# Strassen's products for five pairs of tiles instead of three, and v of thirteen tiles read as float by SyncE

## The chip, the cores and the metric

The kernel runs on one core of one Trainium2 chip. The metric is the time of one execution in microseconds on the device. Engines are named as in the profile: PE (TensorE) multiplies matrices, DVE (VectorE) and ACT (ScalarE) work elementwise and read PSUM, POOL (GpSimd) works elementwise on SBUF and also issues the DMAs that change a type on the way, SP (SyncE) issues the other DMAs.

## The reference

The first half is a linear attention with decay (four batches, eight heads, 768 tokens, heads of 64), the second a feed-forward layer on the 3072 tokens of 512 numbers that come out of it:

```
for t in range(S):
    state = gamma * state + k[t] (outer) v[t]
    y[t] = q[t] @ state / sqrt(D)
x = y, heads side by side            # 3072 x 512
h = x @ w_in                         # 512 x 2048
g = h + sin(alpha * h)**2 / (alpha + 1e-9)
out = g @ w_out                      # 2048 x 512
```

## The kernel before, in words

The 3072 tokens are 24 tiles of 128. `order` is the order in which they are worked on, called P in the code: the first tile of each of the four batches, then the batches in turn. The tiles form ten groups (`sizes` is 4, eight times 2, then 4). Batch 1's last three tiles and the last five tiles of batches 2 and 3, thirteen in all, are "wide": their q, k and v are loaded for the whole batch at once, head by head, in `load_seq`, 64 tokens to a partition row. The other eleven are loaded tile by tile in `load_chunk`. All of these loads change float to bf16 and are issued by GpSimd.

For each tile v is scaled by a decay (`scale_v`, L184), q and k are transposed (`turn`, L294, a transposing DMA issued by SyncE), and the attention is done in chunks: a score matrix q k, masked on VectorE; a product with the state; a product of the masked scores with v; and a state update. `burst` does it for one tile, `pair` (L537) for two. In `pair` PE first writes the product with the state into the PSUM tile y (tag "two"), then the scores of the next tile into pa (tag "pa"), then the products with v into y, then scores of the tile after that into two banks of tag "mm". VectorE then masks pa, adds to the state, and takes y out in two exits, one per tile (`leave`, L560). PSUM has eight banks: four of tag "mm", two in tag "two", two in tag "pa".

The feed-forward part of a group runs in "phases". Phase g runs the up-projection of group g and the down-projection of group g - 1 side by side. A group of two tiles has eight slots in its phase. A `Slot` (L596) makes eight matmuls of 256 columns into a PSUM tile ph (two blocks of 128 of the 2048 hidden numbers, which the code counts as f = 0 to 15), ScalarE takes the sine, two activations, and the square, and VectorE adds s/alpha to ph and writes gT, the hidden numbers as bf16. The down-projection takes gT as the stationary operand and w_out as the moving one, 512 columns, 16 matmuls per tile into a bank po (`ff_out`, L631); VectorE copies po to SBUF and SyncE stores it. `phase` (L878) issues in each slot: the slot's matmuls and activations, what the last attention left to do, the attention at that slot (`atts`), the masks, a share of the down-projection, the slot's addition on VectorE, the second exit, the rest of the masks, and whatever is put behind the slot (`behind_slot`). Every engine works off its instructions in the program's order. The order of the first phases is written out by hand in `PLAN`.

Groups 8 and 9 are "fast" (L653): their down-projection is not done tile by tile. For a pair of tiles it is a product of two by two blocks (two tiles by two halves of the hidden numbers, with two halves by two halves of w_out), and the class `Seven` (L720) does it with Strassen's seven products instead of eight. A product is eight matmuls of 256 columns. The sums of blocks of w_out are made once by `mix_w` (L675; ten operations of 1024 columns), the sums of blocks of gT by `mix_g` (L687) in steps of three operations: s (sums), d (differences) and x, each for a part of the eight blocks m. The products are numbered 1 to 7: 4 and 3 take gT itself and add up in bank a; 5 and 2 take s and add up in bank b; 1 takes x and goes to bank c; 7 and 6 take d and add up further in bank a. Then VectorE (or ScalarE for the first) does: `hold`, a copy of b; `cross` (L783), a + b, stored as one half of the output; `rest` (L794), c - b; and `main` (L798), a + rest, the other half. `cross` has to read a before products 7 and 6 add to it. For group 8 banks a and b are the two halves of tag "two" and c is in "pa"; its pieces are spread evenly over the 16 slots of phase 9, which has no attention. Group 9 is done at the end by `fast_end`.

Buffers are shared by tag, each waiting for the last reader of what was there: gT has two buffers of 16 KB a partition; the ten buffers "qkr" hold q and k of a tile, later the sums of gT and some of w_out.

## Time and profile before

| what | value |
|---|---|
| median of 3 runs | 206.31 us (205.72 to 708.54) |
| the profiled execution, its own time | 207.02 us |
| its span, first to last instruction | 205.2 us |
| busy: PE, DVE, ACT, POOL | 195.2, 161.5, 151.8, 163.2 us |
| granted clock of PE | 0.997 of full speed |
| DMA queue of GpSimd | 80080 packets, 13.38 MB |
| DMA queues of SyncE and others in hardware | 23472 packets, 11.06 MB |

The page of the profile gives busy times per engine, a strip of the span in 40 slices, the chain of work that ended last, and groups of instructions by line. A row of a group has the line, the engine, the operation, output and input with their shapes, how often (x), busy time and mean of one, then the idle time before them and what ended it. Rows of a timeline have the start in the span, the duration, and the instructions merged. PE's matmuls overlap, so their starts tell more than their durations. Phase 6 starts at 122.33 us, phase 7 at 137.62, phase 8 at 152.92, phase 9 at 169.73. The rows of a stretch of time have the busy time of PE, PEld (loading of stationary operands), DVE, ACT and POOL with the count of each, then the clock, the DMA share and GB/s.

### The profile page before, as it was taken

To read this page: it belongs to the slowest core of one execution; us is meant where nothing else is said; L and a number is where in the kernel's file an instruction comes from. 1 tells how busy PE (TensorE), PEld (TensorE's weight loads), DVE (VectorE), ACT (ScalarE), POOL (GpSimd) and SP (SyncE) were. 2 spreads that over 40 slices of the span, in tenths; PEclk is the share of its full clock that TensorE was granted. 3 is DMA by queue.
4 is the path that set the end of the run, shared out by engine and by line. 5 is a ranking of instruction groups with operands and counts; after the bars stand their busy time and mean duration, and the time that the engine had idled before them with its cause. 6 is when DMAs were issued, how large, how long until landed. Compare 5 with 4: busy or idle time off the path is not lost.

```text
span 205.2 us, 6029 instructions
## 1 busy us (share of the span) xinstructions
PE 195.2 (95%) x2426; PEld 131.4 (64%) x2455; DVE 161.5 (79%) x344; ACT 151.8 (74%) x312; POOL 163.2 (80%) x204
## 2 busy tenths in 40 slices
PE   7889999999998999999999999999999999999993
PEld 7444544557765667666666676666766665555983
DVE  5787499877998887887998885995998775577853
ACT  7678888656996877877877959588586869999120
POOL 8998996999999996997399997999193876997000
PEclk9999999999999999999999999999999999999998
DMA  8999999999999999999996796994406101001123
GB/s 133 147 175 192 201 201 176 167 134 106 231 151 188 104 171 194 170 136 150 143 116 117 89 141 117 120 131 104 105 2 107 51 5 51 3 0 51 54 102 102
DMA packets 103580, 24.82 MB, mean 121 GB/s; under 512 B 93392, under 2 KB 101248, under 8 KB 103552
## 3 DMA queue, kind: packets, MB, share of 16 engines
q0 software_dynamic: 80080, 13.38, 92.8%
q1 hardware_dynamic: 23472, 11.06, 26.8%
q8 instruction: 19, 0.31, 0.7%
q14 instruction: 9, 0.07, 0.1%
HBM read 27.30 MB, written 6.29 MB: 164 GB/s over the span
## 4 chain that ended last, share of the span: by engine, by line
PE 83%; DMA 7%; POOL 4%; issue 2%; DVE 2%; ACT 1%; POOLq 0%
PE ph L610 37%; PE po L634 28%; DMA qkT<-qkr 4%; PE a L756 3%; DMA qkr<-in_q_dram 3%; PE ab L756 3%; POOL qkr L125 2%; PE b L756 2%; PE py L373 1%; POOL vr L125 1%; PE c L756 1%; PE pt L291 1%; PE pa L388 1%; PE py L437 1%; POOL w_in L161 1%
## 5 line engine op out<-in xcount | busy, mean ns | idle before, releaser
L625 DVE SCALAR_TENSOR_TENSOR gT<-s,rec_alpha,ph 128x256 bf16<-128x256 f32 (+3 forms) x164 | 79.4, 522 | 25.1 <-ACT s L618 24.6
L610 PE MATMUL ph<-xT,w_in 128*128 128x256 bf16 (+3 forms) x653 | 98.0, 291 | 0.3
L613 ACT ACTIVATE s<-ph,alpha_sb 128x256 f32<-128x256 f32 (+3 forms) x164 | 75.9, 505 | 28.1 <-PE ph L610 26.3
L610 PEld LDWEIGHTS <-w_in 128*128 128x128 bf16 x656 | 63.1, 98 | 29.6 <-DVE s_f L568 0.7
L634 PE MATMUL po<-w_out,gT 128*128 128x512 bf16 x264 | 70.3, 379 | 2.3 <-issue 1.9
L618 ACT ACTIVATE s<-s 128x512 f32<-128x512 f32 (+1 forms) x94 | 58.7, 626 | 2.8
L634 PEld LDWEIGHTS <-gT 128*128 128x128 bf16 x288 | 26.4, 98 | 20.8 <-DVE gT L625 0.5
L710 POOL TENSOR_TENSOR g_mix<-gT 128x512 bf16<-128x512 bf16 (+1 forms) x27 | 25.9, 994 | 7.2 <-DVE gT L625 7.2
L149 POOL DMA_DIRECT2D qk_seq<-in_q_dram x32 | 21.5, 712 | 6.6 <-DMA v_seq<-in_v_dram 6.1
L149 POOL DMA_DIRECT2D qk_seq<-in_k_dram x32 | 21.3, 720 | 1.5 <-DMA qk_seq<-in_q_dram 1.4
L149 POOL DMA_DIRECT2D v_seq<-in_v_dram x24 | 16.8, 743 | 0.0
L681 POOL TENSOR_TENSOR w_mix<-w_out 128x1024 bf16<-128x1024 bf16 x7 | 15.2, 2190 | 0.0
L756 PEld LDWEIGHTS <-g_mix 128*128 128x128 bf16 x128 | 11.9, 98 | 3.6
L644 DVE COPY o_sb<-po 128x512 f32<-128x512 f32 x15 | 10.3, 687 | 2.0 <-PE po L634 1.6
L125 POOL DMA_DIRECT2D vr<-in_v_dram x11 | 10.3, 932 | 1.2 <-DMA w_in<-in_moe_w_in_dram 0.7
L189 POOL TENSOR_TENSOR v_seq<-v_seq,kgq 128x512 bf16<-128x512 bf16 x9 | 9.8, 1097 | 1.4 <-DMA v_seq<-in_v_dram 1.4
L407 DVE TENSOR_TENSOR aTw<-pa,maskq 128x768 bf16<-128x768 f32 x10 | 9.5, 954 | 0.0
L495 DVE TENSOR_TENSOR xT<-py,qg 128x512 bf16<-128x512 f32 x13 | 8.9, 683 | 0.5 <-PE py L453 0.5
L869 PE MATMUL spare<-warm 128*128 128x112 bf16 (+1 forms) x52 | 7.9, 325 | 1.4 <-DVE warm L199 1.2
L391 DVE TENSOR_TENSOR aT<-pa,mask 128x1024 bf16<-128x1024 f32 x7 | 8.5, 1219 | 0.4 <-PE pa L388 0.4
L520 ACT CAST s_q<-s_f 128x256 bf16<-128x256 f32 x13 | 5.1, 393 | 2.7 <-DVE s_f L515 2.7
L165 POOL DMA_DIRECT2D w_out<-in_moe_w_out_dram x8 | 5.8, 727 | 1.2 <-DMA w_in<-in_moe_w_in_dram 0.8
(138 smaller groups left out, 217.7 us busy)
## 6 DMA issues: line engine op xcount, KB each, us to landing
out_dram<-o_sb SPq DMA_DIRECT2D x21, 256.0 KB, 3.9
w_in<-in_moe_w_in_dram POOLq DMA_DIRECT2D x8, 256.0 KB, 8.3
w_out<-in_moe_w_out_dram POOLq DMA_DIRECT2D x8, 256.0 KB, 7.9
vr<-in_v_dram POOLq DMA_DIRECT2D x11, 128.0 KB, 5.3
v_seq<-in_v_dram POOLq DMA_DIRECT2D x16, 80.0 KB, 4.7
qkr<-in_q_dram POOLq DMA_DIRECT2D x7, 128.0 KB, 6.4
qkr<-in_k_dram POOLq DMA_DIRECT2D x7, 128.0 KB, 5.8
qk_seq<-in_q_dram POOLq DMA_DIRECT2D x16, 48.0 KB, 4.4
```

Of the source, the lines that this page charges most:

```text
L125: nc.gpsimd.dma_start(out=t, in_=chunk_of(src, j))
L149: nc.gpsimd.dma_start(out=o, in_=src[bt, head(b, m, e), now[0] * C:(now[-1] + 1) * C, :].rearrange("(f i) d -> i f d", i=64))
L189: eng.tensor_mul(t, t, by[:, j % NCH, :, None].to_broadcast([128, H, D]))
L610: nc.tensor.matmul(self.ph[:, m, :], w_in[:, i, f * 128:(f + 1) * 128], xT[g][:, i, self.lo:self.hi], start=(m == 0 and i == 0), stop=(i = ...
L613: nc.scalar.activation(out=self.s[:, m, :], in_=self.ph[:, m, :], func=ACTF.Sin, scale=alpha_sb[:, f:f + 1])
L618: nc.scalar.activation(out=self.s, in_=self.s, func=ACTF.Square)
L625: nc.vector.scalar_tensor_tensor(gT[self.g][:, f, self.lo:self.hi], self.s[:, m, :], rec_alpha[:, f:f + 1], self.ph[:, m, :], op0=ALU.mult ...
L634: nc.tensor.matmul(po[g, ts], gT[g][:, f, ts * C:(ts + 1) * C], w_out[:, f, :], start=(f == 0), stop=(f == FF - 1))
L644: nc.vector.tensor_copy(o_sb, po[g, ts])
L681: eng.tensor_tensor(w_mix[n, i], w_block(*a, js), w_block(*b, js), op=op)
L710: eng.tensor_tensor(o, i0, i1, op=op)
L756: nc.tensor.matmul(t, self.left(n, j), r, start=k not in self.begun, stop=(j == FH - 1), skip_group_check=True)
```

## The change

1. v of the thirteen wide tiles is read as float, without a change of type, by SyncE. It goes into a new tile vf (16 rows of 256 floats), which takes the tag "gA". Groups 0 and 9, of four tiles, put their gT there too (one buffer of 16 KB); the groups of two keep "gT", two buffers of 8 KB. So vf lies where group 0's gT was, and group 9's gT comes after it. Batch 1 has the first six rows; batches 2 and 3 have the last ten, one after the other. `scale_v` now reads vf and writes the bf16 v. Batch 1's loads come right after PLAN, batch 2's in phase 3, batch 3's in phase 5, in SyncE's queue between transposes and stores.
2. The scalings move: those of tiles 9, 10, 11 and 13 go from VectorE to GpSimd, that of tile 17 comes earlier.
3. Groups 6 and 7 become fast as well: five pairs (groups 6, 7, 8 and two in group 9). Their `mix_g` steps are all on GpSimd, four steps of three operations each, behind slots 1, 3, 5 and 7 of their own phase.
4. Which products run in which slot is written out for groups 6 and 7. Group 6 (in phase 7, with a pair's attention in slot 4): bank a in "mm", banks b and c in "two"; `hold` on ScalarE in slot 3, `cross` and the first half of product 7 in slot 4, product 1 in slots 6 and 7. Group 7 (in phase 8, with a pair's attention in slot 1 and bursts in slots 4 and 6): all banks in "mm"; `hold` in slot 4, `cross` in slot 5, `rest` in slot 6.
5. The sums of w_out are made earlier, in phases 2 to 4: ten halves (512 columns) into the rooms "vr" of early v, seven on VectorE and three on GpSimd; five whole ones on GpSimd, into the rooms of the decay table and of batch 1's q and k.

The diff, cut to its core:

```
 def load_seq(...):
+        if "v" in names and "vf" not in raw:
+            raw["vf"] = work.tile([128, 16, NP, D], F32, name="vf", tag="gA", bufs=1)
...
+            if name == "v":
+                vf = raw["vf"][:, 16 - nh:16] if nh > 6 else raw["vf"][:, 0:nh]
+                for i, c in enumerate(cs):
+                    raw["vf", bt * NCH + c] = vf[:, 2 * i:2 * i + 2]
...
-                nc.gpsimd.dma_start(out=o, in_=...)
+                (nc.sync if name == "v" else nc.gpsimd).dma_start(out=o, in_=...)

 def scale_v(j, eng):
         t, by = raw["v", j], kg
+        o = t
         if wide(j):
-            t, by = t.rearrange("i f p d -> i (f p) d"), kgq
-        eng.tensor_mul(t, t, by[:, j % NCH, :, None].to_broadcast([128, H, D]))
+            o, t = (x.rearrange("i f p d -> i (f p) d") for x in (t, raw["vf", j]))
+            by = kgq
+        eng.tensor_mul(o, t, by[:, j % NCH, :, None].to_broadcast([128, H, D]))

-                gT[g] = work.tile([128, FF, n], BF16, name="gT", tag="gT", bufs=2)
+                gT[g] = work.tile([128, FF, n], BF16, name="gT", tag="gA" if sizes[g] == 4 else "gT", bufs=1 if sizes[g] == 4 else 2)

-    fast = (8, 9)
+    fast = (6, 7, 8, 9)

+    w_todo = {"vr": [(n, j, 2) for n in (7, 6) for j in range(0, FH, 2)] + [(1, 4, 2), (1, 6, 2)],
+              "dec": [(4, 0, 4), (4, 4, 4)], "seq": [(3, 0, 4), (3, 4, 4), (1, 0, 4)]}
+    def mix_w(eng, home):
+        n, i, c = w_todo[home].pop(0)
...
+        eng.tensor_tensor(to, w_block(*a, slice(i, i + c)), w_block(*b, slice(i, i + c)), op=op)

 class Seven:
+        def steps(self, *parts):
+            return [fn for part in parts for fn in ([part] if callable(part) else self.pieces(part))]

 def fast_pieces(g):
+        if g == NG - 3:
+            s = Seven(g, 0, lambda k: psum.tile([128, 2, NH], F32, name=k, tag="mm", bufs=4)[:, slice(0, 2) if k != "c" else 0])
+            parts = [[(4, range(7))], [(4, range(7, FH)), (3, range(6))], [(3, range(6, FH)), (5, range(5))],
+                     [(5, range(5, FH)), (2, range(4))], [(2, range(4, FH)), s.hold], [s.cross, (1, J)], [s.rest, (7, J)],
+                     [(6, J), s.main]]
+            return [s.steps(*p) for p in parts]
+        if g < NG - 3:
+            def between(k):
+                if k == "a":
+                    return psum.tile([128, 2, NH], F32, name=k, tag="mm", bufs=4)
+                return psum.tile([128, 2, 512], F32, name=k, tag="two")[:, 0].rearrange("p (x n) -> p x n", x=2)[:, slice(0, 2) if k == "b" else 0]
+            s = Seven(g, 0, between)
+            parts = [[(4, J)], [(3, J)], [(5, J)], [(2, J), s.hold], [s.cross, (7, range(4))], [(7, range(4, FH)), (6, range(3))],
+                     [(1, range(7))], [(1, range(7, FH)), s.rest, (6, range(3, FH)), s.main]]
+            return [s.steps(*p) for p in parts]

 def phase(...):
+        plan = outs if outs and isinstance(outs[0], list) else None
...
+            for fn in plan[n] if plan else ():
+                fn()

     load_seq(1, "q", between=P[8])
     load_seq(1, "k")
+    load_seq(1, "v")
     load_chunk(P[10], "v")
-    load_seq(1, "v")
     load_seq(2, "q")
+    scale_v(P[11], nc.gpsimd)
+    scale_v(P[12], nc.gpsimd)
     load_seq(2, "k")
-    load_seq(2, "v")
+    scale_v(P[13], nc.gpsimd)
     load_seq(3, "q", slice(0, 2))
     load_seq(3, "k", slice(0, 2))
-    for j in P[15:17] + P[18:19]:
-        scale_v(j, nc.gpsimd)

     def last_loads():
-        mix_w(nc.gpsimd)
         nc.gpsimd.tensor_copy(seen, st["qkT", P[17]][:, 0, 0:1])
         load_seq(3, "v")
-        mix_w(nc.gpsimd)
-        mix_w(nc.gpsimd)
+        load_seq(3, "q", slice(2, None))
         scale_v(P[17], nc.gpsimd)
-        load_seq(3, "qk", slice(2, None))
+        load_seq(3, "k", slice(2, None))

+    at((3, 3), lambda: load_seq(2, "v"))
+    for spot in ((2, 4), (2, 6), (3, 1), (3, 2), (3, 3), (3, 4), (3, 6)):
+        mixes(spot, lambda: mix_w(nc.vector, "vr"))
+    for spot in ((3, 4), (3, 5)):
+        mixes(spot, lambda: mix_w(nc.gpsimd, "dec"))
+    for i, spot in ((14, (3, 6)), (15, (4, 0)), (16, (4, 1)), (18, (4, 2)), (20, (4, 3))):
+        mixes(spot, lambda j=P[i]: scale_v(j, nc.gpsimd))
+    for spot in ((3, 7), (4, 1), (4, 2)):
+        mixes(spot, lambda: mix_w(nc.gpsimd, "vr"))
+    for _ in range(3):
+        mixes((4, 5), lambda: mix_w(nc.gpsimd, "seq"))
+    for g in (6, 7, 8):
+        for m in range(0, FH, 2):
+            mixes((g, m + 1), lambda g=g, m=m: mix_g(g, m, 2, nc.gpsimd))
```

Here (g, n) is slot n of phase g, NG is 10, J is all eight blocks of a product.

More of the change, by code (lines that the diff above doesn't have):

```diff
@@ L147, in load_seq @@
                 r, at = half(b), 2 * m + e
[L148 to L149 removed]
+                o = vf[r, fs, at, :] if name == "v" else tqk[r, fs, "qk".index(name), at, :]
+                (nc.sync if name == "v" else nc.gpsimd).dma_start(out=o, in_=src[bt, head(b, m, e), now[0] * C:(now[-1] + 1) * C, :].rearrange("(f i) d -> i f d", i=64))
         for i, c in enumerate(cs):
@@ L743, in right @@
                 return w_out[:, j + FH * (n == 5), NH * (n == 5):NH * (n == 5) + NH]
-            return w_mix[n, j // 4][:, j % 4]
+            return w_mix[n, j]
         def mm(self, n, j, half=None):
@@ L878, in phase @@
     def phase(g, outs, att, nf=1, on_vector=(), tags={}, early=()):
-        no, done = len(outs), 0
+        plan = outs if outs and isinstance(outs[0], list) else None
+        no, done = 0 if plan else len(outs), 0
         for n in range(FF // nf):
```

38 lines of the change are left out of this document (13 added, 25 removed).

## The prediction

> **What bounds the kernel now.** I read the page first, then PE's busy time by stretches.
>
> ```profile
> span 205.2 us, 6029 instructions
> PE 195.2 (95%) x2426; PEld 131.4 (64%) x2455; DVE 161.5 (79%) x344; ACT 151.8 (74%) x312; POOL 163.2 (80%) x204
> ```
> ```profile
> 60.00:80.00 20.00, 18.39 (x277) 12.91 (x279) 17.65 (x37) 15.30 (x33) 17.34 (x27) 1.00 1.80 161
> ```
>
> TensorE is busy 95% of the span; even the stretch from 60 to 80 us leaves it only 20 - 18.39 = 1.6 us idle. So the time is what PE executes plus what it waits, and relieving another engine buys nothing by itself. What matters is whether PE stays fed where the change touches it: phases 7 and 8, in which groups 6 and 7 go through w_out. The timeline of PE around the pair block of phase 7 comes next (start, duration, instruction).
>
> ```profile
> 142.84 1.04 PE L610 MATMUL ph<-xT,w_in 128*128 128x256 bf16 x8
> 143.71 1.03 PE L634 MATMUL po<-w_out,gT 128*128 128x512 bf16 x4
> 144.57 1.04 PE L610 MATMUL ph<-xT,w_in 128*128 128x256 bf16 x8
> 145.54 0.42 PE L544 MATMUL y<-qkT,s_q 64*64 64x128 bf16 x16
> ...
> 145.96 0.30 PE L421 MATMUL pa<-v_seq,qk_seq 64*64 64x64 bf16 x16
> ...
> 146.84 1.04 PE L634 MATMUL po<-w_out,gT 128*128 128x512 bf16 x3
> ...
> 152.92 1.04 PE L610 MATMUL ph<-xT,w_in 128*128 128x256 bf16 x8
> ```
>
> Slot 3 starts at 142.84, slot 4 at 144.57, the pair's attention at 145.54, phase 8 at 152.92: each starts where the last one ends. Nothing there waits today.
>
> **The products saved.** From 143.71 to 144.57 four passes of 512 columns take 0.86 us, 0.2155 each. The chain of waits has the Strassen passes of 256 columns:
>
> ```profile
> 197.70 1.75 PE a L756 x16
> ```
>
> That is 0.1094 each. A pair needs 32 of the first (6.90 us) or 56 of the second (6.13 us): 0.77 us saved, 1.55 for both pairs. This has one answer. All else is whether it survives.
>
> **Group 6 in phase 7: three new waits.** Slot 3 ends with product 2 and `hold`, ScalarE's copy of bank b; slot 4 has the pair's attention, then `cross`, then product 7 into the bank that `cross` reads; slot 6 opens bank c. Both b and c take the PSUM tag "two", which the pair's y takes as well. The rows that price it, ScalarE's and then VectorE's timeline, then the groups by form:
>
> ```profile
> 144.78 0.63 ACT L618 ACTIVATE s<-s 128x512 f32<-128x512 f32 x1
> ```
> ```profile
> 145.44 0.87 DVE L625 SCALAR_TENSOR_TENSOR gT<-s,rec_alpha,ph 128x256 bf16<-128x256 f32 x2
> 146.32 0.96 DVE L407 TENSOR_TENSOR aTw<-pa,maskq 128x768 bf16<-128x768 f32 x1
> 147.19 0.41 DVE L568 TENSOR_TENSOR s_f<-s_f,pa 128x256 f32<-128x256 f32 x1
> 147.52 0.87 DVE L625 SCALAR_TENSOR_TENSOR gT<-s,rec_alpha,ph 128x256 bf16<-128x256 f32 x2
> ...
> 151.11 0.68 DVE L561 TENSOR_TENSOR xT<-y,qg 128x512 bf16<-128x512 f32 x1
> ```
> ```profile
> L765 ACT COPY b_sb<-b 128x512 f32<-128x512 f32 x2 | 1.2, 585 | 5.2 <-PE b L756 5.2
> L791 DVE TENSOR_TENSOR o_sb<-a,b_sb 128x512 f32<-128x512 f32 x1 | 0.7, 691 | 2.2 <-ACT b_sb L765 2.2
> ```
>
> First, `hold` is queued on ScalarE behind slot 3's square, which ends at 144.78 + 0.63 = 145.41, and lasts 0.585: bank b is free at 146.0. The pair's first matmul, at 145.54 today, needs it: 0.45 us. Bounds 0 and 0.6.
>
> Second, the pair ends at 146.84 + 0.45 = 147.29. VectorE's mask needs the scores and the state sums in pa, ended at 145.96 + 0.30 + 0.45 = 146.71, so it runs then; the state addition follows 0.87 later at 147.58 (147.19 - 146.32), and `cross` 0.33 after that (147.52 - 147.19), at 147.91, since it comes behind both in program order. It ends 0.69 later at 148.60. Product 7 must not write what `cross` still reads: PE stands from 147.29 to 148.60, 1.31 us, with slot 5's matmuls and through them ScalarE queued behind. Bounds 0, were product 7 free of `cross`, and 1.6.
>
> Third, from the addition at 147.52 to the end of the pair's second exit at 151.11 + 0.68 VectorE's chain is 4.27 us today; now it starts at 148.60, so y is released at 152.87. PE does four passes (0.44), slot 5 (0.87), seven passes (0.77) and slot 6 (0.87), which makes 151.55, and finds c not free: 1.32 us. Bounds 0 and 1.9.
>
> The three make 3.1 us. Phase 7 becomes 3.1 - 0.77 = 2.3 us longer; what ends last there is VectorE behind the pair.
>
> **Group 7 in phase 8.** Its banks a, b and c all come from the four of tag "mm". A ph bank is held from 142.84 to the end of its addition, 145.44 + 0.87: 3.47 us. While b lives (slots 2 to 4) two banks are left for slots that come every 0.87 + 7 x 0.109 = 1.63 us, so the same bank is wanted after 3.26: about 0.2 us late, once, as the attention in slots 1, 4 and 6 stretches the others. `cross` stands a whole slot ahead of product 7 here. I take 0.25 us, bounds 0 and 1: so -0.5 net.
>
> **GpSimd.** It issues 24 fewer loads of v; it gains 24 combinations (eight steps of three) and four scalings; the sums of w_out move earlier. Rows: groups, then GpSimd's timeline, then the loads of v by tile.
>
> ```profile
> L710 POOL TENSOR_TENSOR g_mix<-gT 128x512 bf16<-128x512 bf16 x18 | 20.4, 1156 | 7.2 <-DVE gT L625 7.2
> L149 POOL DMA_DIRECT2D v_seq<-in_v_dram x24 | 16.8, 743 | 0.0
> L681 POOL TENSOR_TENSOR w_mix<-w_out 128x1024 bf16<-128x1024 bf16 x7 | 15.2, 2190 | 0.0
> L189 POOL TENSOR_TENSOR v_seq<-v_seq,kgq 128x512 bf16<-128x512 bf16 x9 | 9.8, 1097 | 1.4 <-DMA v_seq<-in_v_dram 1.4
> L710 DVE TENSOR_TENSOR g_mix<-gT 128x512 bf16<-128x512 bf16 x6 | 2.3, 417 | 0.0
> L577 POOL CAST s_q<-s_f 128x512 bf16<-128x512 f32 x2 | 1.4, 694 | 4.5 <-DVE s_f L572 4.5
> ```
> ```profile
> 107.88 3.05 POOL L189 TENSOR_TENSOR v_seq<-v_seq,kgq 128x512 bf16<-128x512 bf16 x3
> ...
> 125.08 1.04 POOL L189 TENSOR_TENSOR v_seq<-v_seq,kgq 128x512 bf16<-128x512 bf16 x1 [1.41 <-DMA v_seq<-in_v_dram]
> 126.06 5.31 POOL L149 DMA_DIRECT2D qk_seq<-in_q_dram  x8
> ...
> 158.22 2.90 POOL L710 TENSOR_TENSOR g_mix<-gT 128x512 bf16<-128x512 bf16 x3 [3.52 <-DVE gT L625]
> ```
> ```profile
> DMA to landing us min/median/max: 2.7/5.1/8.9
> ```
>
> Its first block of loads ends at 107.88 today; without 16 issues of v (11.9 us), with three of the new scalings among them (3.3), at about 99, some us less where waits on v go. Then come five whole sums of w_out (10.9), three halves (3.3) and five scalings (5.5): about 119. The last loads follow: eight of q (5.3) to 124, the scaling of tile 19 when v has landed (125.08 today; I keep that, SyncE having the loads now), and eight of k to 131.4. Only then do group 6's steps start. To the first operation of its last step stand three steps (8.7), a scaling (1.1), the state copy (0.7) and 1.16: 143.1. Product 5 in slot 2 reads it as its seventh pass, at 142.84 - 0.87 + 6 x 0.109 = 142.6. I take 0.5 us. Below: 0, as PE cannot gain from an early one; above: v landing at its 8.9 in place of 5.1, 3.8 more, 4.3. Phases 7 and 8 then ask GpSimd for 4 x 2.9 plus two scalings and a copy, 14.5 us of some 15, so it catches up by phase 9.
>
> GpSimd takes 1156 ns for what VectorE does in 417, 2.8 times. The Trainium skill, GPSIMD Engine Reference, section Engine selection, speaks against this choice: two-input elementwise work belongs on VectorE, GpSimd being some two times slower. By that factor a step would be about a quarter shorter and the 0.5 us would vanish; by the rows it stays.
>
> **SyncE and the loads of v.** SyncE's timeline, and the first use of a wide tile's transposes:
>
> ```profile
> 60.62 0.66 SPq L960 DMA_DIRECT2D out_dram<-o_sb  x1
> 69.16 1.23 SPq L297 DMA_TRANSPOSE qkT<-qk_seq  x1
> ```
> ```profile
> L395 PEld LDWEIGHTS <-qkT x104: 106/108/111, 78.0 to 162.1; 64*64 64x64 bf16 x104
> ```
>
> The first eight loads of v fall into SyncE's gap from 61.3 to 69.16; group 0's gT is dead by then, its last store (60.62) being issued ahead of them. Queued behind them: the transposes of tile 9, wanted at 78.0, and group 1's stores. The gap of 7.9 us takes eight issues at 0.66 (5.3). I take 0, bounds -0.3 (GpSimd's q and k queue gets shorter) and 3. The other sixteen come with 10 us or more ahead of their use. The scalings and sums taken from VectorE, and the three additions per pair that it gets instead of two copies, cost nothing but the waits above.
>
> **Sum.** 3.1 + 0.25 + 0.5 - 1.55 = +2.3 us on the span of 205.2, so 207.5; the profiled execution took 207.02 with what lies around the span, 0.7 above the median of the runs, 206.31. On the median: 208.6.
>
> **Rivals.** (a) The saving comes through: `cross` or the exits don't hold PE, for instance because VectorE, with fewer scalings, reaches them sooner. Against it: VectorE has no gap from 145.44 to 147.52, and each of these comes when PE's own scores are done. It gives -1.55 + 0.25, so 205.0. (b) Slower: GpSimd becomes the bound in phase 7. Its place is the seventh pass of product 5; it decides from 142.6 on, each us later is a us of the kernel, up to 4.3 in place of 0.5: 212.4. For it: the chain from 107.88 has no slack left in it; against: the waits on v that go. (c) SyncE's queue: v's packets ahead of tile 9's transposes make PE stand at 78.0, up to 3 us: 211.6. The Trainium skill, DMA: Bandwidth & Descriptors, section Queues, rings and completion order, says that descriptors of one queue are taken in ring order; no row of before shows such a load ahead of a transpose. (d) The change does not lower PE's work, for instance as 256-column passes pair badly with matmuls of other shapes: 0.1094 was measured at the end of the kernel alone; then +1.55 more, 210.2.
>
> Chances: the forecast 0.52, (a) 0.25, (b) 0.14, (c) 0.05, (d) 0.04. The point is the forecast's. The forecast's own range is 207 to 210.5. The low end takes in (a), 204.8; the high end most of (b) and (c), 212. About 2% (4.1 us) is what a measurement can tell from no change. Faster needs under 202.2: the whole saving and 2.5 us of waits that no row promises, 0.03. Slower needs over 210.4: most of (b) and (c), half of (d), a little of the forecast's tail, 0.22. Within: 0.75.
>
> **What would show it.** In the timeline of PE of after: idle before the pair's y with ScalarE's b_sb as the releaser (0.4), before product 7 with VectorE's o_sb (1.3), before product 1 with VectorE's exit (1.3), and before product 5 with GpSimd's g_mix (0.5); phase 8 lasting about half a us less than the 16.8 from 152.92 to the start of phase 9:
>
> ```profile
> 169.73 1.03 PE L610 MATMUL ph<-xT,w_in 128*128 128x512 bf16 x4
> ```
>
> PE without those gaps, or a gap before 100 us, would make the prediction wrong.

## The result, and the profile after

The changed kernel takes 220.07 us (median of 4 runs, 217.30 to 223.24) against 206.37 us before: a ratio of 1.063, with a 95% interval of 1.0497 to 1.0764. It is clearly slower. A few executions of a kernel come out slower than its others, and the ratios here and below leave these out (708.54 of before, 223.24 of after), so they are not quite the quotients of the medians, and e6's profile is of such an execution. The profiled execution took 217.3 us, with a span of 215.5 us, 10.3 more than the 205.2 before.

The length of a phase is read here from ScalarE's timeline: from the first square (L626; L618 before) of one phase to the first of the next. In the kernel after, phase 7 runs from the first of these rows to the second, 23.9 us:

```profile
141.91 0.63 ACT L626 ACTIVATE s<-s 128x512 f32<-128x512 f32 x1
...
165.81 0.63 ACT L626 ACTIVATE s<-s 128x512 f32<-128x512 f32 x1
```

| us | phase 2 | 3 | 4 | 5 | 6 | 7 | 8 |
|---|---|---|---|---|---|---|---|
| before | 15.89 | 15.67 | 15.58 | 16.31 | 14.99 | 15.30 | 16.64 |
| after | 14.82 | 17.91 | 15.67 | 16.32 | 16.09 | 23.89 | 16.10 |

The page after, in the lines that answer to those of before, and the busy times of 60 to 80 us:

```profile
span 215.5 us, 6176 instructions
...
PE 197.4 (92%) x2479; PEld 137.4 (64%) x2503; DVE 164.0 (76%) x346; ACT 153.0 (71%) x314; POOL 172.4 (80%) x209
```
```profile
60.00:80.00 20.00, 17.58 (x269) 12.21 (x271) 18.91 (x37) 15.22 (x33) 17.19 (x24) 1.00 1.98 177
```

PE is idle for 18.1 us of the span where it was for 10.0 before, and its share fell from 95% to 92%: 8.1 of the 10.3 us are waiting. The other 2.2 are PE being busy longer. From phase 9 on nothing moved (18.67 us to the last square in both). So 8.6 of the 10.3 us are in phase 7, 2.2 and 1.1 in phases 3 and 6, and phases 2 and 8 give back 1.1 and 0.5. From 60 us on, the rows of PE's timeline with a wait of over 0.3 us (in brackets: the idle time and what ended it) say who was late:

```profile
78.56 0.30 PE L454 MATMUL py<-aT,vr 64*64 64x128 bf16 x8 [1.57 <-DVE vr L197]
...
79.31 0.25 PE L403 MATMUL pa<-qkT 64*64 64x128 bf16 x4 [0.38 <-DMA qkT<-qk_seq]
...
132.93 0.37 PE L445 MATMUL y<-aTw,v_seq 64*64 64x128 bf16 x16 [0.67 <-POOL v_seq L197]
...
146.84 0.39 PE L764 MATMUL b<-w_out,g_mix 128*128 128x256 bf16 x2 [1.73 <-POOL g_mix L718]
149.66 0.39 PE L764 MATMUL b<-w_out,g_mix 128*128 128x256 bf16 x2 [2.42 <-POOL g_mix L718]
...
156.99 0.60 PE L764 MATMUL a<-w_mix,g_mix 128*128 128x256 bf16 x4 [1.35 <-DVE o_sb L799]
...
161.56 0.94 PE L764 MATMUL c<-w_mix,g_mix 128*128 128x256 bf16 x7 [1.46 <-DVE xT L569]
```

The last two are the waits for `cross` and for bank c, as forecast. The two before them are product 5 waiting for GpSimd's sums, 4.15 us together. Behind them PE also ran slower; the column before the last two is the granted clock:

```profile
140.00:150.00 10.00, 5.84 (x51) 4.52 (x50) 4.16 (x9) 5.19 (x11) 10.00 (x12) 1.00 0.22 54
...
150.00:160.00 10.00, 8.65 (x164) 6.90 (x161) 5.46 (x12) 5.00 (x10) 8.63 (x10) 0.83 0.23 54
```

Read by the microsecond, the clock is 0.50 to 0.52 from 150 to 153 us, right behind the two waits, and PE is busy all that time: it cost 1.7. Phase 7 then is 15.30 - 0.77 + 4.15 + 1.35 + 1.46 + 1.7 = 23.2. Most of the other 0.7 belongs to the waits too. A wait is counted from the end of the last matmul, but matmuls overlap: the four passes at 144.51 take 0.60 us, where a next one that was free would start 4 x 0.1094 = 0.44 us after them. So a wait costs up to 0.17 us more than its idle time, some 0.6 for the four (an estimate from such rows).

Why GpSimd was late is in the chain of waits, followed back from 149.66 (start, us, what):

```profile
112.25 6.26 POOL w_mix L687 x3
118.51 0.14 POOL seen L1122
...
118.66 0.63 SPq L155
...
121.47 1.90 SPq L155
...
123.42 1.11 SPq L155
...
125.75 5.96 DMA vf<-in_v_dram
...
131.83 1.04 POOL v_seq L197
...
138.40 2.91 POOL g_mix L718 x3
...
149.66 0.39 PE b L764 x2
```

It goes back to SyncE's loads, and they were late in two ways. They started late: batch 3's eight loads of v are issued from 118.66 on, while GpSimd issued them from 113.67 in the kernel before:

```profile
113.67 5.76 POOL L149 DMA_DIRECT2D v_seq<-in_v_dram  x8
```

In SyncE's queue they stand behind tile 16's transposes, whose issue ends at 118.12, and the chain has the first of them behind GpSimd's small copy `seen`, which comes after three whole sums of w_out. And they took longer: the first four issues take some 0.65 us each, the later ones 1.1 to 1.9, and the last load lands at 131.71. From the first issue to the scaling of tile 19 it is 13.17 us, against 125.08 - 113.67 = 11.41 before. So of the 6.75 us by which that scaling was late, 5.0 are the start and 1.8 the loads. GpSimd, which stands still for 7.93 us for that load, scales tile 19 at 131.83 instead of 125.08 before, issues k, and begins group 6's steps at 138.32. SyncE's three batches of such loads:

```profile
60.98 6.20 SPq L155 DMA_DIRECT2D vf<-in_v_dram  x8
...
80.31 12.49 SPq L155 DMA_DIRECT2D vf<-in_v_dram  x8
...
118.66 8.29 SPq L155 DMA_DIRECT2D vf<-in_v_dram  x8
```

And VectorE's timeline in phase 3, then GpSimd's: the scaling of tile 8 for which PE waited at 78.56 took 2.75 us, where the same operation took 0.68 before, and GpSimd made two scalings beside it.

```profile
75.76 2.75 DVE L197 TENSOR_TENSOR vr<-vr,kg 128x512 bf16<-128x512 bf16 x1
```
```profile
75.89 2.05 POOL L197 TENSOR_TENSOR v_seq<-vf,kgq 128x512 bf16<-128x512 f32 x2
```

The transposes of tile 9, for which PE waited at 79.31, were issued at 73.85, 4.7 us later than before. SyncE's queue was free of v from 67.18 on; what SyncE waited for was batch 1's k. In this stretch the median from issue to landing of GpSimd's q and k loads is 5.9 us, where it was 4.1.

### The profile page after: what moved, and what is told of

Its sections match the earlier page's. It is cut to its first block, busy times and chain, and to the rows that moved or that the text cites. A ratio compares the mean times of both kernels' runs of the same rounds, so it can differ in the third digit from the quotient of the medians.

```text
span 215.5 us, 6176 instructions
## 1 busy us (share of the span) xinstructions
PE 197.4 (92%) x2479; PEld 137.4 (64%) x2503; DVE 164.0 (76%) x346; ACT 153.0 (71%) x314; POOL 172.4 (80%) x209
## 4 chain that ended last, share of the span: by engine, by line
POOL 39%; PE 31%; DMA 16%; DVE 4%; SPq 3%; ACT 3%; issue 2%; POOLq 0%; DVEq 0%
PE ph L618 14%; POOL w_mix L687 6%; PE a L764 5%; POOL g_mix L718 4%; POOL qkr L123 4%; POOL qkr L125 4%; DMA qk_seq<-in_q_dram 4%; DMA w_in<-in_moe_w_in_dram 4%; POOL qk_seq L155 4%; POOL vr L125 4%; PE po L642 4%; POOL v_seq L197 3%; DMA vr<-in_v_dram 3%; SPq L155 3%; DMA vf<-in_v_dram 3%; PE b L764 3%
## 5 line engine op out<-in xcount | busy, mean ns | idle before, releaser
L618 PE MATMUL ph<-xT,w_in 128*128 128x256 bf16 (+3 forms) x652 | 98.9, 292 | 0.4
L618 PEld LDWEIGHTS <-w_in 128*128 128x128 bf16 x656 | 63.7, 98 | 26.7 <-issue 0.7
L626 ACT ACTIVATE s<-s 128x512 f32<-128x512 f32 (+1 forms) x94 | 58.7, 626 | 2.9
L642 PE MATMUL po<-w_out,gT 128*128 128x512 bf16 x206 | 54.8, 379 | 2.0 <-issue 1.6
L718 POOL TENSOR_TENSOR g_mix<-gT 128x512 bf16<-128x512 bf16 (+1 forms) x51 | 49.1, 1008 | 6.6 <-DVE gT L633 5.3
L642 PEld LDWEIGHTS <-gT 128*128 128x128 bf16 x224 | 20.6, 98 | 16.5 <-DVE gT L633 0.5
L764 PEld LDWEIGHTS <-g_mix 128*128 128x128 bf16 x208 | 19.8, 100 | 12.9 <-POOL g_mix L718 4.7
L155 POOL DMA_DIRECT2D qk_seq<-in_k_dram x32 | 21.3, 697 | 1.9 <-DMA qk_seq<-in_q_dram 1.6
L197 POOL TENSOR_TENSOR v_seq<-vf,kgq 128x512 bf16<-128x512 f32 x13 | 13.6, 1054 | 7.9 <-DMA vf<-in_v_dram 7.9
L687 POOL TENSOR_TENSOR w_mix<-w_out 128x1024 bf16<-128x1024 bf16 (+1 forms) x8 | 14.0, 1760 | 0.0
L764 PE MATMUL b<-w_out,g_mix 128*128 128x256 bf16 x64 | 9.5, 292 | 4.2 <-POOL g_mix L718 4.2
L125 POOL DMA_DIRECT2D vr<-in_v_dram x11 | 10.3, 934 | 1.0 <-DMA w_in<-in_moe_w_in_dram 0.7
L764 PE MATMUL a<-w_mix,g_mix 128*128 128x256 bf16 (+1 forms) x72 | 8.2, 261 | 1.4 <-DVE o_sb L799 1.4
L764 PEld LDWEIGHTS <-gT 128*128 128x128 bf16 x88 | 7.9, 98 | 2.2 <-DVE gT L633 0.3
L764 PE MATMUL a<-w_mix,gT 128*128 128x256 bf16 (+1 forms) x72 | 8.7, 261 | 0.0
```

Source lines behind the costliest of these rows:

```text
L125: nc.gpsimd.dma_start(out=t, in_=chunk_of(src, j))
L155: (nc.sync if name == "v" else nc.gpsimd).dma_start(out=o, in_=src[bt, head(b, m, e), now[0] * C:(now[-1] + 1) * C, :].rearrange("(f i) d ...
L197: eng.tensor_mul(o, t, by[:, j % NCH, :, None].to_broadcast([128, H, D]))
L618: nc.tensor.matmul(self.ph[:, m, :], w_in[:, i, f * 128:(f + 1) * 128], xT[g][:, i, self.lo:self.hi], start=(m == 0 and i == 0), stop=(i = ...
L626: nc.scalar.activation(out=self.s, in_=self.s, func=ACTF.Square)
L642: nc.tensor.matmul(po[g, ts], gT[g][:, f, ts * C:(ts + 1) * C], w_out[:, f, :], start=(f == 0), stop=(f == FF - 1))
```

## The experiments

Eighteen kernels, e1 to e18 in the order in which they ran ("the seventh run" is e7). Each row has the median in us, the ratio to the kernel before with its interval, the span of the profiled execution, and the lengths of its phases, read as above.

| run | median | ratio [95%] | span | 2 | 3 | 4 | 5 | 6 | 7 | 8 |
|---|---|---|---|---|---|---|---|---|---|---|
| e1 | 217.07 | 1.050 [1.043, 1.057] | 215.8 | 15.82 | 17.87 | 15.67 | 16.31 | 20.56 | 18.11 | 16.10 |
| e2 | 210.40 | 1.019 [1.012, 1.025] | 208.7 | 14.62 | 19.53 | 15.67 | 16.32 | 15.94 | 15.30 | 16.64 |
| e3 | 218.13 | 1.060 [1.051, 1.068] | 215.5 | 15.75 | 17.52 | 15.67 | 16.32 | 22.50 | 16.84 | 16.10 |
| e4 | 218.15 | 1.055 [1.047, 1.063] | 216.9 | 15.38 | 19.71 | 15.68 | 16.33 | 22.31 | 15.93 | 16.10 |
| e5 | 212.28 | 1.029 [1.020, 1.038] | 210.4 | 15.35 | 19.49 | 15.67 | 16.32 | 14.87 | 18.19 | 16.13 |
| e6 | 223.90 | 1.084 [1.077, 1.091] | 224.4 | 15.72 | 24.75 | 15.67 | 16.31 | 16.75 | 23.92 | 16.10 |
| e7 | 214.78 | 1.041 [1.034, 1.048] | 213.5 | 15.57 | 24.60 | 15.67 | 16.32 | 14.87 | 15.93 | 16.10 |
| e8 | 232.03 | 1.126 [1.117, 1.136] | 231.3 | 14.62 | 21.10 | 15.68 | 19.74 | 24.41 | 25.22 | 16.15 |
| e9 | 215.34 | 1.044 [1.039, 1.049] | 212.8 | 14.62 | 15.67 | 21.81 | 16.31 | 17.14 | 15.93 | 16.09 |
| e10 | 227.57 | 1.100 [1.092, 1.107] | 226.3 | 15.47 | 17.16 | 26.17 | 16.32 | 14.87 | 23.92 | 16.12 |
| e11 | 213.94 | 1.037 [1.033, 1.042] | 212.1 | 15.49 | 15.67 | 21.27 | 16.31 | 16.86 | 15.30 | 16.09 |
| e12 | 211.90 | 1.027 [1.023, 1.031] | 210.2 | 14.82 | 15.67 | 15.59 | 16.51 | 20.84 | 15.93 | 16.10 |
| e13 | 211.69 | 1.026 [1.022, 1.029] | 210.2 | 15.01 | 15.67 | 15.59 | 17.37 | 20.68 | 15.30 | 16.10 |
| e14 | 220.18 | one run | 218.4 | 15.83 | 20.87 | 15.58 | 16.32 | 15.19 | 23.91 | 16.13 |
| e15 | 208.43 | 1.010 [1.006, 1.015] | 205.9 | 15.06 | 15.67 | 15.59 | 16.41 | 16.55 | 15.93 | 16.10 |
| e16 | 207.76 | 1.004 [1.001, 1.008] | 204.5 | 14.77 | 15.67 | 15.58 | 16.35 | 16.04 | 15.30 | 16.10 |
| e17 | 206.87 | 1.004 [1.001, 1.007] | 204.9 | 15.43 | 15.67 | 15.58 | 16.32 | 14.87 | 16.47 | 16.10 |
| e18 | 205.83 | 0.998 [0.995, 1.001] | 203.5 | 14.62 | 15.67 | 15.59 | 16.41 | 14.87 | 15.30 | 16.09 |

### Group 6's waits, one at a time: e1, e3, e4

e1 issues batch 3's last k ahead of tile 19's scaling, so that GpSimd doesn't stand idle for v. e3 adds a bank of tag "mm" for c, e4 adds `cross` ahead of the masks.

```
 e1:
-        scale_v(P[17], nc.gpsimd)
         load_seq(3, "k", slice(2, None))
+        scale_v(P[17], nc.gpsimd)
 e3, as well (banks of group 6):
-                if k == "a":
+                if k in ("a", "c"):   # tag "mm"
 e4, as well (in phase 7):
+            if g == 7:
+                for fn in plan[n]:
+                    fn()
             run(fresh, "mask", "keep0")
```

> GpSimd's scaling of tile 19 stands behind the last eight loads of k instead of ahead of them; nothing else moves. Late GpSimd (it stood 7.9 us for v with k and all of group 6's combinations queued behind): the first combination starts at about 133 instead of 138.3, the waits of product 5 (1.7 and 2.4 us) go, and with them the slower clock behind them (0.91 between 140 and 160), some 1.5 us; the copy of b becomes a wait of about 0.4 again. Span about 210.2 from 215.5. If instead the banks or the loads themselves carry the loss, the span stays over 214.

> As e1, and group 6's bank c comes from the four small banks instead of the room of y. The wait of product 1 for the pair's second exit (1.46 us) goes: span 1.4 below e1, about 208.8. If VectorE behind the pair is what PE waits for anyway, the wait only moves to the next slot's bank and the span is that of e1.

> As e3, and in phase 7 the pieces of the down-projection come ahead of the pair's mask in VectorE's order, so that cross no longer stands behind mask and state addition. The wait of product 7 (1.35 us) goes: span 1.3 below e3, about 207.5. If cross is held by something else (the copy of b on ScalarE), the span is that of e3.

Product 5's wait went in all three, and phase 7 fell to 18.11, 16.84 and 15.93 us. PE's timeline of e1:

```profile
135.11 0.37 PE L445 MATMUL y<-aTw,v_seq 64*64 64x128 bf16 x16 [1.26 <-POOL v_seq L197]
...
137.88 0.25 PE L403 MATMUL pb<-qkT 64*64 64x128 bf16 x4 [2.40 <-DMA qkT<-qk_seq]
...
154.54 0.42 PE L552 MATMUL y<-qkT,s_q 64*64 64x128 bf16 x16 [0.32 <-ACT b_sb L773]
157.26 0.60 PE L764 MATMUL a<-w_mix,g_mix 128*128 128x256 bf16 x4 [1.35 <-DVE o_sb L799]
161.83 0.94 PE L764 MATMUL c<-w_mix,g_mix 128*128 128x256 bf16 x7 [1.46 <-DVE xT L569]
```

With GpSimd in time the three bank waits stand there as forecast: 0.32, 1.35, 1.46 (forecast 0.45, 1.31, 1.32). e3 took the third away and gained 1.27 us in phase 7, e4 the second and gained 0.91, since a wait of 0.32 us for the state's addition came in its place. But the total did not fall: v was as late as in the kernel after, and k was now loaded beside it, so phase 6 was 5.6 to 7.5 us longer than before, on tile 19's v, on transposes (tile 20's in e1) and on a lower clock behind these waits (0.50 to 0.67 from 138 to 142 us in e1). The expected span of 210.2 for e1 was wrong: the loss had only moved one phase up.

### The loads alone, and the loads once more by GpSimd: e2, e8

e2 has all of the change but the two pairs: groups 6 and 7 are done tile by tile, without their `mix_g` steps. e8 gives the float loads of v back to GpSimd's queue and keeps all else.

```
 e2:
-    fast = (6, 7, 8, 9)
+    fast = (8, 9)
 e8:
-                (nc.sync if name == "v" else nc.gpsimd).dma_start(out=o, in_=...)
+                nc.gpsimd.dma_start(out=o, in_=...)
```

> Groups 6 and 7 are done tile by tile again; v by SyncE, the moved scalings and the early sums of w_out stay. If the loss sits in the two added pairs, phase 7 is back at 15.3 us and phase 8 at 16.8, and only the early waits of the profile after stay (1.57 + 0.38 at 78 us, 0.67 at 133): span 207.8. If SyncE's loads slow everything down, it stays at 213 or more.

> The changed kernel with v read as float by GpSimd's queue at the same places of the program; SyncE issues none of it. If SyncE's queue is the culprit, tile 19's v lands by 126 and product 5's waits go. If GpSimd's order is the bound, 24 issues of 0.7 us (17 us) in front of the combinations make them later than in the profile after, and phase 7 is longer than its 23.9 us; span over 222.

e2 still costs 3.5 us of span: phases 7 and 8 are those of before, phase 3 is 3.9 us longer and phase 6 1.0. So moving loads and scalings, priced at nothing, has a price without any Strassen product of groups 6 and 7. Its waits in phase 3 (1.67 us for VectorE's scaling, 0.45 for transposes) are only a little longer than in the kernel after, but here the clock fell. The rows of 80 to 85 us, before and then e2:

```profile
80.00:85.00 5.00, 5.00 (x36) 3.33 (x35) 4.07 (x9) 4.09 (x10) 5.00 (x8) 1.00 2.15 173
```
```profile
80.00:85.00 5.00, 4.67 (x27) 2.87 (x27) 3.58 (x8) 1.93 (x5) 5.00 (x7) 0.77 1.68 194
```

That is the profiled execution of e2, with a span of 208.7 us. Two others kept a mean clock of 1.00 and had spans of 208.5 and 207.5, so most of the price isn't the clock's.

e8 is far slower than the kernel after: with v in its queue GpSimd is late everywhere (PE waits 3.24 and 7.93 us for scaled v, 4.5 for product 5). So with all of v on GpSimd this order of work is worse still; taking v off it was not free either.

### The last loads earlier, the first ones later: e5, e6, e7

e5 issues batch 3's v three slots earlier, scales tile 19 behind k, and makes the three whole sums of w_out later. e6 issues batch 1's v behind the transposes of tiles 9 and 10, at slot 6 of phase 2; its three scalings and the first q and k of batch 3 move behind it. e7 is both, with e3's bank and e4's order.

```
 e5:
+    at((5, 2), lambda: load_seq(3, "v"))
 def last_loads():
-        load_seq(3, "v")
...
 e6:
-    load_seq(1, "v")
+    at((2, 6), middle_loads)   # load_seq(1, "v") and the three scalings
```

> The changed kernel with the last v issued by SyncE three slots earlier (phase 5, slot 2, ahead of tile 16's transposes), and GpSimd's three whole sums of w_out behind the last loads of q and k instead of ahead of them (the third behind group 6's combinations). If the loss of phases 6 and 7 comes from loads that crowd at 118 to 134 us, with the combinations waiting behind them, phase 6 is back at about 15.1 us (16.1 after) and phase 7 has the three bank waits alone: 17.6 to 18.1, as in e1 (18.1), from 23.9; span about 208.7. If GpSimd has too much work in any order, product 5 still waits for its combinations and phase 7 stays over 20.

> The changed kernel with batch 1's v issued by SyncE after the transposes of tiles 9 and 10 (phase 2, slot 6) instead of ahead of them, and the three scalings that read it behind batch 2's q and k on GpSimd. If v in SyncE's queue ahead of the transposes is what phase 3 pays for (17.9 us against 15.7 before), phase 3 goes back to 15.7 and the span falls by about 2.2, less what phases 6 and 7 make of another timing. If only the scalings on GpSimd beside VectorE's scaling (2.75 us instead of 0.68) matter, the transposes' wait grows in its place and phase 3 stays over 17.

> e5 and e6 together with the two bank changes of e3 and e4. Phases: 2 and 3 as before, 6 at 15.1, 7 at 14.9 (15.3 less 0.77, with the copy of b still a wait), 8 at 16.1: span about 204.3, 1 us below the kernel before. If Strassen's products for groups 6 and 7 cannot be fed beside that attention, it stays over 207.

e5 confirmed phases 6 and 7: 14.87 us, and 18.19 with the three bank waits alone. e6's expectation fell. PE did not wait for transposes any more, but 6.45 us for v itself (6.56 in e7), as its eight issues now began at 75 to 76 us, beside GpSimd's loads of batch 2. e7 shows how far phase 7 comes down, 15.93 us: 0.63 more than tile by tile, with waits of 0.32, 0.32 and 0.20 us left. With some 0.17 us for each restart that is 15.30 - 0.77 + 0.84 + 0.5 = 15.9: three short waits cost more than the 0.77 that the products save. A pair by Strassen's products in group 6 saved nothing, in any of these orders.

### Batch 1 back to GpSimd: e9, e11, and VectorE beside GpSimd: e10, e14

e9 is e7 with batch 1's v loaded as bf16 by GpSimd and scaled by VectorE, as before the change. e11 is e9 with group 6 tile by tile (four pairs). e10 and e14 are the kernel after, with only the scalings of tiles 9 to 11 given back to VectorE; e14 has the last of them, tile 11's, two slots earlier than e10. (The expectations of e10, e12 and e14 count scalings and transposes by place in the order of work: their tiles 13 and 14 are tiles 11 and 13, and e10's scaling that took 2.75 us is tile 8's.)

```
 e9, e11:
+            fl = name == "v" and bt > 1
...
-                (nc.sync if name == "v" else nc.gpsimd).dma_start(out=o, in_=...)
+                (nc.sync if fl else nc.gpsimd).dma_start(out=o, in_=...)
 e9, e10, e11:
-    for i, spot in ((9, (2, 3)), (10, (3, 0))):
+    for i, spot in ((9, (2, 3)), (10, (3, 0)), (11, (3, 3)), (12, (3, 7)), (13, (4, 3))):
 e14:
+    for i, spot in ((9, (2, 3)), (10, (3, 0)), (11, (3, 3)), (12, (3, 7)), (13, (4, 1))):
```

> Theory: what is left of the loss after the seventh run (phase 3, 24.6 us there) belongs to batch 1's v alone, which SyncE loads ahead of tile 9's transposes and GpSimd scales beside VectorE. Here GpSimd loads that v as bf16 again and VectorE scales it, as in the kernel before; batches 2 and 3 stay with SyncE, and phases 6 to 8 are those of the seventh run. So phases 2 and 3 take the 15.9 and 15.7 us of before, phases 6, 7 and 8 take 14.9, 15.9 and 16.1, and the span is 205.2 us, that of before, since -0.1 + 0.6 - 0.5 = 0. Rival: the sums of w_out that VectorE makes in phases 2 and 3, or batch 2's v on SyncE in phase 3, cost there too; then phase 3 stays above 16.5 us and the span above 206.5.

> The kernel after, but the three scalings of batch 1's float v go back to VectorE, at the slots that they had before; all else stays. Theory: two causes overlap at the start of phase 3, VectorE's scaling of tile 9 (2.75 us beside GpSimd's two scalings, 0.68 alone) and tile 9's transposes behind the eight loads of v; each alone holds PE until about the same time. So the scaling returns to 0.7 us, the wait for it goes, and the wait for the transposes grows to about 1.9 us; phases 2 and 3 together stay at 32.5 to 34.5 us. Rival: the scaling is the cause and the transposes wait only in consequence; then PE waits under 0.5 us and phase 3 takes 16.2 us or less. Phase 7 stays above 21 us by both, as tile 19's v lands no earlier.

> The ninth run with group 6 done tile by tile again, so that four pairs of tiles are done by Strassen's products (groups 7, 8 and two in 9); bank c and cross, which only group 6 had moved, are as in the kernel after. Theory: group 6's pair costs 0.6 us more than it saves, even with every mendable wait gone, and group 7's saves 0.5; so phase 7 is 15.3 us, phase 8 16.1, phase 6 14.9, and the span 204.5 us, 0.7 under the kernel before, if phase 3 is as before. Rival: GpSimd's sums or SyncE's loads still cost in phases 3 to 6, then the span is 205.2 or more.

> The tenth run with one move: tile 13's scaling by VectorE at slot 1 of phase 4 in place of slot 3, where it took 9.22 us, from 100.98 to 110.20, while GpSimd ran eight sums and scalings one behind the other from 99.22 to 109.64. Theory: a VectorE operation with both inputs in SBUF makes no headway while GpSimd works elementwise without a pause, whatever its own length; one slot pair earlier GpSimd is still issuing loads, so the scaling takes 0.69 us, PE's wait of 7.89 us for o_sb goes, phase 4 takes 15.7 to 17 us in place of 26.2, and the span is about 10 us less than the 226.3 there. Rival: the scaling was long for its float input, or as v landed late; then it takes well over 1 us in its new place too.

e9 and e11: phase 3 is back at 15.67 us, so its loss was batch 1's v, its loads and its scalings together. But the span stayed at 212.8 and 212.1, against the expectation: phase 4 now takes 21.8 and 21.3. PE's timeline of e9, then SyncE's:

```profile
104.30 0.32 PE L404 MATMUL pa<-qkT 64*64 64x128 bf16 x4 [3.54 <-DMA qkT<-qk_seq]
```
```profile
78.11 13.63 SPq L156 DMA_DIRECT2D vf<-in_v_dram  x8
...
100.49 1.27 SPq L306 DMA_TRANSPOSE qkT<-qk_seq  x1
```

Batch 2's eight issues took 13.63 us, beside GpSimd's q and k of the same batch. Its k (the row of DMA issues with eight of 80 KB; the last number is the median from issue to landing), before and then in e9:

```profile
qk_seq<-in_k_dram POOLq DMA_DIRECT2D x8, 80.0 KB, 4.4
```
```profile
qk_seq<-in_k_dram POOLq DMA_DIRECT2D x8, 80.0 KB, 10.0
```

So tile 13 could be transposed only at 100.49, 9.6 us later than before, where SyncE's timeline has:

```profile
90.85 1.23 SPq L297 DMA_TRANSPOSE qkT<-qk_seq  x1
```


e10's rival had no case in phase 3, where the scaling took 0.68 us again and the wait for the transposes grew to 1.40. But a new loss of 10 us came in phase 4. VectorE's timeline of e10, then GpSimd's:

```profile
100.98 9.22 DVE L197 TENSOR_TENSOR v_seq<-vf,kgq 128x512 bf16<-128x512 f32 x1
```
```profile
99.22 4.21 POOL L687 TENSOR_TENSOR w_mix<-w_out 128x1024 bf16<-128x1024 bf16 x2
103.40 1.03 POOL L197 TENSOR_TENSOR v_seq<-vf,kgq 128x512 bf16<-128x512 f32 x1
...
108.61 1.03 POOL L197 TENSOR_TENSOR v_seq<-vf,kgq 128x512 bf16<-128x512 f32 x1
113.71 1.16 POOL L687 TENSOR_TENSOR w_mix<-w_out 128x512 bf16<-128x512 bf16 x1 [4.07 <-PE pa L429]
```

VectorE's scaling ended 0.56 us after GpSimd's eight operations paused (109.64). In e14 the same scaling stands two slots earlier, while GpSimd issues loads:

```profile
99.09 0.68 DVE L197 TENSOR_TENSOR v_seq<-vf,kgq 128x512 bf16<-128x512 f32 x1
```

Phase 4 is 15.58 us in place of 26.17. So it is no property of the float input: this scaling, an operation with both inputs in SBUF, gets nowhere while GpSimd works elementwise without a pause. (e14's phase 3, 20.87 us, has a wait of 3.55 us for tile 9's transposes and a clock of 0.83 from 80 to 90 us: batch 1's v is still loaded by SyncE there.)

### The loads apart in time: e12, e13, e15, e16, e17, e18

e12 is e9 with batch 2's v behind tile 13's transposes. e15 also reorders GpSimd's work so that batch 3's v has the DMA engines for itself. e17 puts tile 19's scaling between the last q and k again. e13, e16 and e18 are the same three with group 6 tile by tile, as in e11.

```
 e12:
-    at((3, 3), lambda: load_seq(2, "v"))
+    at((3, 6), lambda: load_seq(2, "v"))
 e15, as well: scalings of batch 2 behind the three half sums, whole sums ahead of the last q and k
-    for i, spot in ((14, (3, 6)), (15, (4, 0)), (16, (4, 1)), (18, (4, 2)), (20, (4, 3))):
+    for i, spot in ((14, (4, 3)), (15, (4, 3)), (16, (4, 3)), (18, (4, 4)), (20, (4, 4))):
...
-        mixes((5, 6), lambda: mix_w(nc.gpsimd, "seq"))
+        mixes((4, 5), lambda: mix_w(nc.gpsimd, "seq"))
 e17, as well:
+        scale_v(P[17], nc.gpsimd)
         load_seq(3, "k", slice(2, None))
-        scale_v(P[17], nc.gpsimd)
```

> The ninth run with batch 2's v issued by SyncE at slot 6 of phase 3, behind tile 14's transposes, and tile 13's scaling on VectorE at slot 1 of phase 4 in place of slot 3. Theory: the DMA engines are what is full (the strip of their share reads 9 in nearly every slice up to 110 us, before as after), so a load that SyncE takes over isn't had for nothing, it pushes back what runs beside it; in the ninth run that was batch 2's k, whose median from issue to landing went from 4.4 us (before) to 10.0, and with it tile 14's transposes, for which PE waited 3.54 us and then had a lower clock. With v behind k, k takes 4 to 6 us again, phase 4 takes 15.7 us in place of 21.8, phase 6 15.0 in place of 17.1, and the span is 204.4 to 205.3 us. Rival: k is late for another reason, the order of GpSimd's own issues; then tile 14's transposes still hold PE by 2 us or more and phase 4 stays above 18 us.

> The same two moves in the eleventh run, that is with group 6 tile by tile and four pairs by Strassen's products. By the theory phase 4 goes from 21.3 to 15.7 us, phase 6 from 16.9 to 14.9, phase 7 stays at 15.3, phase 8 at 16.1, and the span is 204.5 us, some 0.7 below the kernel before: that is group 7's gain. By the rival phase 4 stays above 18 us and the span above 207.

> The twelfth run with GpSimd's work in another order: three half sums of w_out in place of its wait of 3.59 us for batch 2's v, then the five scalings, then the three whole sums, and only then the last loads of q and k, so that batch 3's v on SyncE (which in the twelfth run went out from 115.28 to 123.82 beside GpSimd's q, and pushed the pair's transposes to 131.88 and PE's wait of 4.05 us) has the DMA engines for itself. Theory: it is two loads at a time that makes SyncE's issues long; apart they take under 6.5 us, the pair's transposes are issued by about 128, phase 6 takes 15 to 16.3 us in place of 20.8, phases 2 to 5, 7 and 8 stay, and the span is 204.4 to 206 us. Rival: SyncE's eight issues are long by themselves, and the transposes wait behind them wherever they stand; then phase 6 stays above 18 us and the span above 207.5. That product 5 waits again for GpSimd, whose steps begin at about 130, costs up to 1 us by either.

> The same order with group 6 tile by tile (four pairs by Strassen's products). By the theory phases 5 and 6 take 16.3 and 15 to 16.3 us in place of 17.4 and 20.7, phases 7 and 8 stay at 15.3 and 16.1, and the span is 204 to 205.5 us, at or just below the kernel before. By the rival phase 6 stays above 18 us and the span above 207.5.

> The fifteenth run with the scaling of batch 3's first wide v between the last loads of q and those of k again, where the kernel after has it. That v is there from about 119 us now, so the scaling runs at about 123 in place of 130.45, and the wait of 1.49 us in phase 6 goes: phase 6 takes 14.9 to 15.3 us in place of 16.55, and the span is 204.3 to 204.8 us, 0.4 to 0.9 below the kernel before. That would show the sum for five pairs once no load is late. Rival: the k loads then end later by the scaling and by waits, and either tile transposes or product 5 wait for them; then the span stays at 205.9.

> The sixteenth run with the same move. Phase 6 takes 14.9 to 15.3 us in place of 16.04, and the span is 203.4 to 203.8 us, 1.4 to 1.8 below the kernel before: about 0.5 of it is group 7's pair, the rest what phases 2 and 6 gain as v's loads leave GpSimd. Rival as there: the span stays at 204.5.

In e12 and e13 phase 4 is that of before (15.59 us; e12's k lands after 5.3), so the theory held there. What was expected of the whole did not: phase 6 took 20.8 and 20.7, now behind batch 3's v. e15 has the same loads earlier and alone. SyncE's and PE's timelines of e12, with the transposes of tile 16 for which PE waits at 133.69 (they landed 8.8 us after their issue; the row at 131.88, which the expectation of e15 names, is tile 17's), then the same of e15:

```profile
115.28 8.54 SPq L156 DMA_DIRECT2D vf<-in_v_dram  x8
...
124.81 3.41 SPq L306 DMA_TRANSPOSE qkT<-qk_seq  x1
```
```profile
133.69 0.25 PE L404 MATMUL pa<-qkT 64*64 64x128 bf16 x4 [4.05 <-DMA qkT<-qk_seq]
```
```profile
111.50 5.58 SPq L156 DMA_DIRECT2D vf<-in_v_dram  x8
...
118.08 1.63 SPq L306 DMA_TRANSPOSE qkT<-qk_seq  x1
```
```profile
131.62 0.37 PE L446 MATMUL y<-aTw,v_seq 64*64 64x128 bf16 x16 [1.49 <-POOL v_seq L198]
```

Alone, eight issues take 5.58 us, 0.70 each, close to the 0.66 of the prediction; beside GpSimd's loads they took 6.2 to 13.6. So the rival, that they are long by themselves, fell. But e15 also starts them 3.8 us earlier, as GpSimd's scalings of batch 2, which free the room of that v, end at 111.48 in place of 115.25. Tile 16's transposes go out 6.7 us earlier, 3.0 from the shorter issues and 3.8 from the start; the run does not tell the two apart, and by these numbers either would take off most of the 4.05 us. The transposes are no longer late, and e15's last wait is for tile 19's scaling, which stood behind k. e17 and e18 moved that and phase 6 is 14.87 us. In e17 the forecast of 204.3 to 204.8 was missed by 0.1, as product 5 waits 0.37 us for GpSimd again (its steps begin at 131.18).

So with every load in time five pairs take 206.87 us against 206.50 before, a ratio of 1.004 that lies just above 1 (1.001 to 1.007), and four pairs 205.83: a ratio of 0.998 whose interval, 0.995 to 1.001, holds 1. e18's span is 1.7 us shorter, but 1.3 of that is phase 2, which varies by itself: e1 to e5 and the kernel after have the same instructions up to there, and their profiles show 14.6 to 15.8 us. The profile of before, with a wait of 1.14 us for transposes, stands at that range's long end. What is left for the change is phase 8's 0.5 us, too little to show between these medians.

## Why the prediction was wrong

Right in mechanism and size:
- **The pair of group 7.** Phase 8 was to be 0.5 us shorter; it is 0.54 shorter, in the kernel after and in all runs with that pair.
- **The three waits of group 6.** 0.45, 1.31 and 1.32 us were forecast; e1 and e5 show 0.32, 1.35 and 1.46 to 1.55. In the kernel after the first is hidden, as ScalarE idled while PE waited for product 5.
- **Rival (a)** had no case: the saving of group 6 did not come through even with most of those waits gone (e4, e7).

Wrong:
- **GpSimd, 0.5 us: this is the step that failed.** It kept the time of 125.08 at which v of tile 19 was there in the kernel before, since SyncE has the loads now. That v landed at 131.71, and GpSimd stood still for it from 123.9 on, though the loads of batches 2 and 3 were to come "with 10 us or more ahead of their use". The chain that was then drawn (q, scaling, k, three steps, first operation of the fourth) held: its 143.1, put 131.83 - 125.08 = 6.75 later, is 149.85, and PE went on at 149.66. What failed is when the load starts, 5.0 us later than by GpSimd before, and how long it takes, 1.8 us more. The prediction put GpSimd's last loads of q at about 119, which came out (118.58), but did not ask when SyncE's loads of v would go out. e5, which issues them from 112.29, has neither of product 5's waits; it moves other work too. Rival (b) had this mechanism, with 0.14. It allowed v a delay of 3.8 us, not 6.75; the wait stayed at 4.15, within its 4.3, because PE itself came some 2.5 us later to that product (145.1, against 142.6). Its total of 212.4 left out the lower clock (1.7), the restarts (0.6) and the losses in phases 3 and 6 (3.3).
- **SyncE, "I take 0".** It counted eight issues at 0.66 us, the price of one store, and asked whether the queue had room. The queue had: the first eight took 6.20 us in a gap of 7.9. The DMA engines had not. The strip of their share (40 slices of the span, before and then after) is a line of the page that the prediction did not read:

```profile
DMA  8999999999999999999996796994406101001123
```
```profile
DMA  9999999999999999999632999930042502001123
```

It reads 9 in nearly every slice up to some 100 us, before as after, and in the kernel after again from 118 to 140, where batch 3's v is loaded. A load that another queue takes over there is paid by whatever it runs beside: batch 1's k and with it tile 9's transposes (phase 3), batch 2's k (e9, phase 4), the pair's transposes (phase 6, e1, e12). e12 shows it from the other side for batch 2, moved behind tile 13's transposes: its k is back at 5.3 us. In e18, with batch 1's v back on GpSimd and batch 3's alone, phases 3 to 6 are those of before within 0.12 us. The Trainium skill, DMA: Bandwidth & Descriptors, section Issuing engines are not separate DMA queues, says just that: DMAs of all issuing engines run on the same 16 engines, and issuing from several saves only the sequencer's time. The trace agrees, with 5.58 us for eight issues alone and 13.63 beside GpSimd's. The prediction drew on that page for the order within a queue only.
- **Rival (c)** saw the place (tile 9's transposes) and put 3 us on it at most, with 0.05. Its mechanism, the order within SyncE's queue, was not what held them: the queue was free of v 6.7 us before their issue, and they waited for batch 1's k. The waits in phase 3 were 1.57 and 0.38 us, and the first was VectorE's scaling of tile 8 behind GpSimd's scalings, a cost for which the prediction had no term: it counted GpSimd's added scalings on GpSimd alone. With that scaling in time (e10) the wait for the transposes is 1.40, so the two lay on top of each other.
- **The clock and the restarts** were in no term. A wait was priced at its idle time.

Together: the span was to grow by 2.3 us and grew by 10.3. The 8.0 us between are product 5's wait (4.15 in place of 0.5), the clock (1.7), the restarts (0.6), phase 3 (2.2) and phase 6 (1.1), less phase 2 (1.1), which varies by itself, and some 0.2 in smaller terms.

The chance given to a time above 210.4 us was 0.22. The errors were not independent: loads that came late moved three terms in the same direction, and the range added them as if each had its own luck.

## What to carry to other kernels

When a load moves to another queue, work out anew when it can start: what stands ahead of it there, and who still reads the room that it fills. Its landing time in the old queue says nothing of that. Before a transfer is moved to another queue, read the strip of the DMA engines' share at the place where it will run: where it reads 9, ask which load beside it will land later and who waits for that. A saving of 0.8 us in TensorE's work is not worth a dependence on a second engine's order unless every wait that it adds ends with room to spare. Put such scalings of VectorE, with two inputs in SBUF, where GpSimd issues DMAs, not where it computes.
